# Queries as evicted serve head B's scores: mask rows on both halves, keys written from PSUM into the operands, and a planner that holds loads back

## The chip, the cores and the metric

The kernel runs on one core of a Trainium2 chip. The metric is the device time of one execution in microseconds (us), and the number that counts is the median over the runs. The engines are TensorE (PE; PEld is its weight load), VectorE (DVE), ScalarE (ACT), GpSimd (POOL) and SyncE (SP), which here only issues DMAs.

## The reference

Two stages. First an attention over blocks: q, k and v are [4, 8, 768, 64] in float32 (4 batches, 8 heads, 768 positions, width 64). Keys are averaged over blocks of 64; each query scores the 12 block means, and keeps the three best among the blocks that are not ahead of its own, and its own block. Ordinary causal softmax attention then runs over the kept blocks alone:

```
gate = q . mean(k, block of 64);  sel = top 3 of the causal blocks, and the own block
attn = softmax(where(sel & causal, q.k / 8, -1e9)) v
```

Then the heads are put side by side (x is [4, 768, 512]) and go through a gated long convolution over the sequence:

```
x1, x2, x3 = split(x @ w_proj)                    # w_proj [512, 1536]
y = x1 * irfft(rfft(x2) * rfft(filter)) * x3      # along the 768 positions
out = y @ w_out                                   # [4, 768, 512] float32
```

The Fourier transforms are done as matmuls with sine tables.

## The kernel before, in words

**Groups.** The work is 16 groups of two heads (A and B, `t` = 0 and 1), four groups to a batch. `prep(g)` makes a group ready, `attn(g)` does its attention, `hyena(b)` does the convolution of a batch once its four groups are through. Work of several groups runs interleaved.

**What `prep` does.** SP loads q, k (two transfers each) and v. PE transposes k and q in 128x128 pieces (L480, L517) into PSUM, so that the 64 partitions 0 to 63 hold head A and 64 to 127 head B, with the 768 positions along the row. DVE sums the blocks of keys (L485), ACT casts the keys to fp16 into `k2` (L490), POOL splits the sums in a high and a low half (`km`, L498, L499). ACT writes the scaled queries in fp16 as `q2h` (L522), DVE what rounding left as `q2l` (L527). PE multiplies both with `km` (the gate, L548). DVE finds the third largest of each row and writes a 0/1 mask (`sel`, L560 to L576); PE transposes the mask (L584); DVE copies it out of PSUM (L588).

**The operands of the scores.** A "slot" holds a group's score operands, and there are four slots. `Kt[i]` and `Qt[i]` are [128, 2, 768] in fp16; head `t` is the plane `[:, t, :]`, of which rows 0 to 63 are keys or queries and rows 64 to 75 the mask: in `Kt` a fixed pattern (-30720 where the row's number is the key's block, written once, L294), in `Qt` the mask of the group (L588). A matmul over 76 rows then gives the score and, where a block is not kept, a large negative number beside it (L606). The planes need head B's keys and queries on partitions 0 to 63, while the transposes left them on 64 to 127; and `k2` and `q2h` are used by the gate too. So both heads are copied into the planes: for the first six groups (`direct=6`) POOL copies the keys (L505, two to a group) and DVE the queries (L535, two to a group); from the seventh on SP moves both with DMAs from SBUF to SBUF (L503, L533, four to a group).

**What `attn` does.** For each head, PE computes scores into six PSUM banks (L606), ACT takes the exponential (L614), POOL zeroes above the diagonal (L625, "tri"), PE multiplies with v and a column of ones (L636, "pv"), DVE divides (L647, L648) into `xn`. `xn` is then folded by POOL (L676) and Fourier transformed by PE (L682); and its transpose goes to `xT`, for the first four groups (`xpe=4`) by PE with a DVE copy (L664, L670), later by a DMA transpose that SP issues (L655).

**What `hyena` does.** PE multiplies the transform with the middle of w_proj ("w2", L718), DVE with the filter's transform (L727), POOL combines (L732 to L748), PE transforms back (L788) and computes x1 and x3 from `xT` (L764); DVE and POOL multiply (L777, L800, L806); PE multiplies with w_out (L817), ACT or DVE evicts (L824), SP stores. Before the first `hyena`, the filter is loaded (six SP transfers, L374), POOL adds and subtracts its halves (six TENSOR_TENSOR, L382 and L385, "the six sums"), PE transforms it (L399, L406).

**What sets the order.** Nothing is scheduled on the chip. `Graph.schedule` (L104) is a planner that runs in Python: every operation has an engine, a duration that is written beside it, a priority and its dependencies, and the planner takes in turn the one that can start first, smaller priority first. What comes out is the order in which each engine's instructions are written, and an engine runs them strictly in that order, waiting where an operand is not there. SP's transfers are in the plan too, with `dma_free`, the time at which it believes the DMA queues to be empty. Group g is to start at `T(g)` = 9 + 13.6 g us, its `prep` 1.75 groups ahead. `f_at`, and the `after=` of the weight loads that POOL issues (L429, L434), say from which planned time on a load may go.

## Time and profile before

| | |
|---|---|
| runs | 261.70, 259.53 and 261.67 us; median 261.67 |
| the profiled execution | 259.5 us, of which the span from the first to the last instruction is 257.8 |
| mean granted TensorE clock | 0.975 of full speed |
| busy, us | PE 231.6, DVE 181.1, ACT 177.4, POOL 181.7, PE's weight loads 148.6 |
| DMA | 35.55 MB moved, 138 GB/s over the span |

The busy times are shares of one whole execution. PE is busy for 90% of the span; the 10% that are missing lie at the two ends: from about 79 us to 240 us PE hardly stops. Numbers behind a row in the form "x12" are counts of instructions; "mean ns" is the mean of one; what stands last in a row of the groups is the idle time of that engine just ahead of these instructions, and who ended it.

### The profile page before, as it was taken

The page shows a single profiled execution, that of the slowest core. Times are in us where ns is not written, and L with a number is a line of the kernel's source. Part 1 is how long each engine was busy: PE and PEld are TensorE (multiplying, and loading weights), DVE is VectorE, ACT ScalarE, POOL GpSimd, SP SyncE. Part 2 cuts the span into 40 slices and gives each one's busy share as a digit, 9 for nine tenths or more (in the row PEclk, how much of TensorE's full clock was granted, in tenths as well). Part 3 has the DMA queues.
Part 4 walks back from the last instruction along what each step waited for, and adds up shares of the span by engine and source line. Part 5 has one row for each costly group of instructions (what it writes and reads, how often), then busy time and mean ns, then how long its engine had stood idle before and what let it go on. Part 6 is the DMA issues. An engine that isn't in the chain of part 4 may idle for free.

```text
span 257.8 us, 6443 instructions
## 1 busy us (share of the span) xinstructions
PE 231.6 (90%) x2255; PEld 148.6 (58%) x2255; DVE 181.1 (70%) x564; ACT 177.4 (69%) x420; POOL 181.7 (70%) x273
## 2 busy tenths in 40 slices
PE   8778942997799999999999999999999999999971
PEld 4456722566476666667556657676655666455420
DVE  7789998359999876677749857767687446872422
ACT  7899980996687866958867966689759774033520
POOL 7556899196696899883917997675659978476550
PEclk9999985899999999999999999999999999999998
DMA  8999999999888293997887729302632011000435
GB/s 163 218 219 213 288 180 222 202 219 164 194 185 109 53 205 85 159 212 144 207 215 199 154 64 157 82 11 65 197 137 36 0 33 31 3 0 0 164 126 202
DMA packets 94272, 35.55 MB, mean 138 GB/s; under 512 B 85792, under 2 KB 90400, under 8 KB 94240
## 3 DMA queue, kind: packets, MB, share of 16 engines
q1 hardware_dynamic: 92128, 33.04, 60.7%
q0 software_dynamic: 2112, 2.10, 5.2%
q8 instruction: 18, 0.29, 0.5%
q14 instruction: 14, 0.11, 0.1%
HBM read 24.64 MB, written 6.29 MB: 120 GB/s over the span
## 4 chain that ended last, share of the span: by engine, by line
PE 52%; DVE 17%; POOL 13%; issue 8%; ACT 7%; DMA 1%; SPq 0%; DVEq 0%; POOLq 0%; ACTq 0%
PE ps L764 11%; PE ps L606 7%; PE ps L718 7%; PE ps L817 5%; PE ps L636 5%; PE ps L788 4%; PE ps L682 4%; POOL Y L748 3%; POOL ex L625 3%; ACT ex L614 2%; PE ps L517 2%; DVE m L568 2%; DVE Qt L588 2%; DVE Qt L535 2%; DVE q2l L527 2%
## 5 line engine op out<-in xcount | busy, mean ns | idle before, releaser
L614 ACT ACTIVATE ex<-ps 128x512 f16<-128x512 f32 x192 | 91.8, 603 | 14.8 <-PE ps L606 12.6
L606 PE MATMUL ps<-Qt,Kt 76*128 76x512 f16 (+3 forms) x256 | 49.3, 308 | 1.8 <-DVE Qt L588 0.8
L764 PE MATMUL ps<-xT,wp 128*128 128x384 f16 x256 | 46.8, 326 | 0.1
L625 POOL TENSOR_SCALAR_AFFINE_SELECT ex<-ex 128x384 f16<-128x384 f16 x64 | 32.4, 522 | 19.3 <-ACT ex L614 17.8
L636 PEld LDWEIGHTS <-ex 128*128 128x128 f16 x672 | 28.2, 98 | 12.7 <-POOL ex L625 4.7
L806 POOL TENSOR_TENSOR yT<-prod,sd 128x768 f16<-128x768 f32 x16 | 28.9, 1812 | 9.0 <-DVE sd L800 7.9
L636 PE MATMUL ps<-va,ex 128*128 128x65 f16 x672 | 31.2, 194 | 2.4 <-POOL ex L625 1.6
L676 POOL TENSOR_TENSOR xeo<-xn 128x384 f16<-128x384 f16 x32 | 28.5, 910 | 5.3 <-DVE xn L648 5.3
L764 PEld LDWEIGHTS <-wp 128*128 128x128 f16 x256 | 23.7, 97 | 14.0 <-issue 0.2
L606 PEld LDWEIGHTS <-Kt 76*128 76x128 f16 x256 | 23.0, 98 | 15.0 <-issue 2.3
L773 ACT CAST x<-ps 128x384 f16<-128x384 f32 x32 | 16.0, 505 | 20.7 <-PE ps L764 12.6
L490 ACT CAST k<-ps 128x384 f16<-128x384 f32 x32 | 15.9, 534 | 16.1 <-DVE ks L485 8.9
L777 DVE TENSOR_TENSOR prod<-ps,x 128x384 f32<-128x384 f32 x32 | 17.1, 553 | 12.8 <-ACT x L773 8.1
L800 DVE TENSOR_TENSOR sd<-ce,ps 128x384 f32<-128x384 f32 x32 | 16.3, 548 | 13.8 <-ACT ce L795 12.2
L817 PE MATMUL ps<-wo,yT 128*128 128x512 f16 x96 | 23.2, 379 | 1.8 <-POOL yT L806 1.7
L718 PE MATMUL ps<-wp,Xf 128*128 128x512 f16 x96 | 23.0, 379 | 0.1
L527 DVE SCALAR_TENSOR_TENSOR q2l<-ps,q2h 128x384 f16<-128x384 f32 x32 | 16.7, 551 | 6.0 <-ACT q2h L522 5.8
L682 PE MATMUL ps<-F,xeo 128*128 128x384 f16 x96 | 20.0, 326 | 0.3 <-DVE q2l L527 0.2
L727 DVE TENSOR_TENSOR t<-ps,HA 128x512 f32<-128x512 f32 x24 | 16.4, 684 | 3.9 <-PE ps L718 3.0
L824 ACT COPY osb<-ps 128x512 f32<-128x512 f32 x21 | 12.8, 613 | 9.0 <-issue 3.8
L788 PE MATMUL ps<-G,Y 128*128 128x384 f16 x96 | 18.9, 326 | 0.0
L648 DVE TENSOR_TENSOR xn<-ps,rec 128x384 f16<-128x384 f32 x32 | 17.8, 557 | 1.2
(99 smaller groups left out, 433.2 us busy)
## 6 DMA issues: line engine op xcount, KB each, us to landing
kn<-in_k_dram SPq DMA_DIRECT2D x32, 192.0 KB, 4.4
qn<-in_q_dram SPq DMA_DIRECT2D x32, 192.0 KB, 4.5
vn<-in_v_dram SPq DMA_DIRECT2D x16, 384.0 KB, 5.1
out_dram<-osb SPq DMA_DIRECT2D x24, 256.0 KB, 2.3
Kt<-k SPq DMA_DIRECT2D x20, 96.0 KB, 3.2
Qt<-q2h SPq DMA_DIRECT2D x20, 96.0 KB, 3.1
t<-in_moe_filter_fft_dram SPq DMA_DIRECT2D x6, 256.0 KB, 5.2
wp<-in_moe_w_proj_dram POOLq DMA_DIRECT2D x3, 512.0 KB, 8.6
```

The lines of the kernel that those rows point to most:

```text
L527: X.nc.vector.scalar_tensor_tensor(out=X.q2l[q2l.slot][:, cs], in0=X.ps(ps)[:, 0:HS], scalar=QS, in1=X.q2h[q2h.slot][:, cs], op0=ALU.mult, ...
L606: X.nc.tensor.matmul(X.ps(ps)[:, col:col + w], lhsT=kt[0:76, t, P * kc:P * (kc + 1)], rhs=qt[0:76, t, q0:q0 + w], start=True, stop=True, s ...
L614: X.nc.scalar.activation(X.ex[ex.slot][:, 512 * i:512 * i + w], X.ps(ps)[:, 0:w], AF.Exp, scale=ESC)
L625: X.nc.gpsimd.affine_select(out=dv, in_=dv, compare_op=ALU.is_ge, fill=0.0, base=0, pattern=[[0, 3], [1, P]], channel_multiplier=-1)
L636: X.nc.tensor.matmul(pt[:, 65 * c:65 * c + 65], lhsT=X.ex[ex.slot][:, w:w + P], rhs=X.va[va.slot][:, t, kc, :], start=(kc == 0), stop=(kc ...
L676: X.nc.gpsimd.tensor_tensor(X.xeo[xeo.slot][:, z, :], v[:, 0:HS], v[:, HS:S], op=a)
L682: X.nc.tensor.matmul(X.ps(ps)[:, 0:HS], lhsT=X.xeo[xeo.slot][:, z, P * t:P * (t + 1)], rhs=X.F[:, t, HS * z:HS * (z + 1)], start=(t == 0), ...
L718: X.nc.tensor.matmul(X.ps(ps), lhsT=l, rhs=X.wp[:, j, Dm:2 * Dm], start=(j == 0), stop=(j == DC - 1))
L764: X.nc.tensor.matmul(X.ps(ps)[:, 0:HS], lhsT=X.wp[:, d2, Dm * base + P * dc:Dm * base + P * (dc + 1)], rhs=X.xT[xT.slot][:, d2, hs:hs + HS ...
L788: X.nc.tensor.matmul(X.ps(ps)[:, 0:HS], lhsT=X.Y[Y.slot][:, 3 * par + n_, P * dc:P * (dc + 1)], rhs=X.G[:, 3 * par + n_, :], start=(n_ == ...
L806: X.nc.gpsimd.tensor_mul(X.yT[yT.slot][:, dc, :], X.prod[prod.slot], X.sd[sd.slot])
L817: X.nc.tensor.matmul(X.ps(ps), lhsT=X.yT[yT.slot][:, d2, P * c:P * (c + 1)], rhs=X.wo[:, d2, :], start=(d2 == 0), stop=(d2 == DC - 1), ski ...
```

## The change

- **One set of operands for both uses.** `Kt`, `Qt`, `k2` and `q2h` go. A slot now has `KA`, `QA` for head A and `KB`, `QB` for head B, each [128, 768] fp16. ACT writes the queries of both heads from PSUM into `QB` (L522): head B's are on rows 64 to 127, where `QB` wants them, and head A's are on rows 0 to 63. The gate reads `QB` too. Head A's queries are copied from `QB` into `QA`: for the first four groups (`direct=4`) by POOL, later by one DMA (L532, L535 of the changed kernel).
- **Mask rows on either side.** `QA` has its mask on rows 64 to 75, as before. `QB` has it on rows 0 to 11, over head A's queries, once these have been copied and the gate has read them (new memset L589, copy L590). `KB` has the fixed pattern on rows 0 to 11 and zeros on the rest of rows 0 to 63, so that what is left of head A's queries counts for nothing. Head B's score matmuls go over 128 rows, head A's over 76 as before. The two halves of `km` and of the mask change places to fit.
- **Keys from PSUM into the operands.** ACT casts head A's half (64 partitions) into `KA`, DVE head B's into `KB` (L496). The copies and DMAs of the keys go.
- **The planner** lets no SP transfer go while it believes the queues to be more than 2.7 us behind. This adds no wait to the program: it changes the order in which SP issues.
- **Numbers.** `xpe=0`: all 16 transposes to `xT` go by DMA. The filter is loaded from planned time 26 us on instead of 14; the weights from T(2.0), T(2.6), T(2.7) and T(3.6) on instead of T(1.0), T(1.6), T(1.7) and T(2.6).

```diff
@@ schedule
+                    if o.dma is not None and e == SP:
+                        t = max(t, dma_free - 2700.0)
                     t = max(t, f)
@@
-POOLS = dict(ps=8, slot=4, kn=3, qn=3, vn=2, va=3, k2=2, q2h=2, q2l=2, ks=2, km=3, nmp=2, m8=2,
+POOLS = dict(ps=8, slot=4, kn=3, qn=3, vn=2, va=3, q2l=2, ks=2, km=3, nmp=2, m8=2,
@@
-def build(X, tau=13.6, ahead=1.75, lag=1.5, direct=6, xpe=4, fill_to=13.0, f_at=14000):
+def build(X, tau=13.6, ahead=1.75, lag=1.5, direct=4, xpe=0, fill_to=13.0, f_at=26000, w_at=2.0):
...
         def qz(i=i):
-            X.nc.vector.memset(X.Qt[i][64:76, :, 0:P], 0.0)
-        op(DVE, 130, qz, w=[tok("slot0", i)], prio=-97 + 0.1 * i)
+            X.nc.vector.memset(X.QA[i][64:76, 0:P], 0.0)
+            X.nc.vector.memset(X.KB[i][0:64, :], 0.0)
+        op(DVE, 500, qz, w=[tok("slot0", i)], prio=-97 + 0.1 * i)
...
-            def kc(cs=cs, ps=ps):
-                X.nc.scalar.copy(X.k2[k2.slot][:, cs], X.ps(ps)[:, 0:HS])
-            op(ACT, act_n(HS), kc, r=[(ps, 0)], w=[(k2, hf)], prio=pr)
+            for t in range(2):
+                def kc(cs=cs, ps=ps, t=t):
+                    r = slice(64 * t, 64 * t + 64)
+                    (X.nc.vector.tensor_copy if t else X.nc.scalar.copy)(
+                        (X.KB if t else X.KA)[sl.slot][r, cs], X.ps(ps)[r, 0:HS])
...
-        for t in range(2):
-            def ksh(t=t):
-                X.nc.sync.dma_start(X.Kt[sl.slot][0:64, t, :], X.k2[k2.slot][64 * t:64 * t + 64, :])
-            def kcp(t=t):
-                X.nc.gpsimd.tensor_copy(X.Kt[sl.slot][0:64, t, :], X.k2[k2.slot][64 * t:64 * t + 64, :])
...
-        for t in range(2):
-            def qsh(t=t):
-                X.nc.sync.dma_start(X.Qt[sl.slot][0:64, t, :], X.q2h[q2h.slot][64 * t:64 * t + 64, :])
-            def qcp(t=t):
-                X.nc.vector.tensor_copy(X.Qt[sl.slot][0:64, t, :], X.q2h[q2h.slot][64 * t:64 * t + 64, :])
...
+        def qsh():
+            X.nc.sync.dma_start(X.QA[sl.slot][0:64, :], X.QB[sl.slot][0:64, :])
+
+        def qcp():
+            X.nc.gpsimd.tensor_copy(X.QA[sl.slot][0:64, :], X.QB[sl.slot][0:64, :])
+        e = (POOL, 850, qcp) if g < direct else (SP, 450, qsh)
+        op(*e, r=[(sl, "q", 0), (sl, "q", 1)], w=[(sl, "qA")], dma=None if g < direct else 430,
+           prio=pr + 40, name="qA")
...
             def mcp(t=t):
-                X.nc.vector.tensor_copy(X.Qt[sl.slot][64:76, t, P:S],
-                                        X.ps16(mt)[64 + 32 * t:76 + 32 * t, 0:S - P])
+                r = slice(64 - 64 * t, 76 - 64 * t)
+                if t:
+                    X.nc.vector.memset(X.QB[sl.slot][r, 0:P], 0.0)
+                X.nc.vector.tensor_copy((X.QB if t else X.QA)[sl.slot][r, P:S], X.ps16(mt)[r, 0:S - P])
...
-               w=[(sl, "m", t)], prio=pr + 60, name="mcp")
+               w=[(sl, "m", t)] + ([(sl, "q", 0), (sl, "q", 1), (sl, "qA")] if t else []),
+               prio=pr + 60, name="mcp")
...
                 def qk(bank=bank, ps=ps, t=t):
-                    kt, qt = X.Kt[sl.slot], X.Qt[sl.slot]
+                    kt, qt = (X.KB, X.QB) if t else (X.KA, X.QA)
+                    r = slice(0, P if t else 76)
                     for (col, kc, q0, w) in bank:
                         X.nc.tensor.matmul(X.ps(ps)[:, col:col + w],
-                                           lhsT=kt[0:76, t, P * kc:P * (kc + 1)],
-                                           rhs=qt[0:76, t, q0:q0 + w], start=True, stop=True,
+                                           lhsT=kt[sl.slot][r, P * kc:P * (kc + 1)],
+                                           rhs=qt[sl.slot][r, q0:q0 + w], start=True, stop=True,
```

How the order moves is shown at three places. The first is DVE, where the fourth group's selection stands. Before (`Qt_81` is the fourth slot; the digits are buffer numbers):

```order
L527 SCALAR_TENSOR_TENSOR q2l_105<-ps_62,q2h_103 128x384
L527 SCALAR_TENSOR_TENSOR q2l_105<-ps_65,q2h_103 128x384
L535 COPY Qt_81<-q2h_103 64x768 x2
L560 MEMSET ps_68 64x5x2
L561 MEMSET ps_68 128x2x8
L562 MEMSET ps_68 128x2x6
L568 MAX m_1_114<-ps_68 128x8 x10
```

and with the change:

```order
L489 TENSOR_REDUCE ks_111<-ps_66 128x6
L496 CAST KB_81<-ps_66 64x384
L527 SCALAR_TENSOR_TENSOR q2l_109<-ps_68,QB_89 128x384
L527 SCALAR_TENSOR_TENSOR q2l_109<-ps_64,QB_89 128x384
L559 MEMSET ps_64 64x5x2
L560 MEMSET ps_64 128x2x8
L561 MEMSET ps_64 128x2x6
L567 MAX m_1_118<-ps_64 128x8 x10
```

The two copies of the queries between the rounding rest and the selection are gone; a cast of the keys stands ahead instead.

The second is POOL, around the six sums of the filter. Before:

```order
L505 COPY Kt_77<-k_1_101 64x768
L382 TENSOR_TENSOR Y_138<-t_130,t_131 128x512
L385 TENSOR_TENSOR Y_138<-t_130,t_131 128x512
L382 TENSOR_TENSOR Y_138<-t_132,t_133 128x512
L385 TENSOR_TENSOR Y_138<-t_132,t_133 128x512
L382 TENSOR_TENSOR Y_138<-t_134,t_135 128x512
L385 TENSOR_TENSOR Y_138<-t_134,t_135 128x512
L505 COPY Kt_77<-k_1_101 64x768
L625 AFFINE_SELECT ex_115<-ex_115 128x3x128 x2
```

and with the change:

```order
L535 COPY QA_85<-QB_89 64x768
L681 TENSOR_TENSOR xeo_128<-xn_125 128x384 x2
L507 CAST km_112<-ks_111 64x12
L508 TENSOR_TENSOR km_112<-ks_111,km_112 64x12
L507 CAST km_112<-ks_111 64x12
L508 TENSOR_TENSOR km_112<-ks_111,km_112 64x12
L630 AFFINE_SELECT ex_119<-ex_119 128x3x128 x2
L387 TENSOR_TENSOR Y_142<-t_134,t_135 128x512
L390 TENSOR_TENSOR Y_142<-t_134,t_135 128x512
L387 TENSOR_TENSOR Y_142<-t_136,t_137 128x512
```

The sums still stand in one run of six, now behind the diagonal mask of a head instead of ahead of it.

The third is SP, behind the six loads of the filter. Before:

```order
L374 DMA t_135<-in_moe_filter_fft_dram 128x512
L454 DMA vn_96<-in_v_dram 128x12x64
L447 DMA kn_91<-in_k_dram 128x6x64 x2
L447 DMA qn_94<-in_q_dram 128x6x64 x2
L447 DMA kn_89<-in_k_dram 128x6x64 x2
L447 DMA qn_92<-in_q_dram 128x6x64
```

and with the change:

```order
L379 DMA t_139<-in_moe_filter_fft_dram 128x512
L660 DMA_TRANSPOSE xT_130<-xn_125 128x6x128
L452 DMA kn_99<-in_k_dram 128x6x64
L452 DMA qn_102<-in_q_dram 128x6x64 x2
L660 DMA_TRANSPOSE xT_130<-xn_126 128x6x128
L532 DMA QA_82<-QB_86 64x768
L459 DMA vn_104<-in_v_dram 128x12x64
L452 DMA kn_97<-in_k_dram 128x6x64 x2
```

Two transposes, of the first and the second group (`xn_125`, `xn_126`), now stand ahead of loads and of the first copy into `QA` by DMA.

More of the change, by code (lines that the diff above doesn't have):

```diff
@@ L282, in etiny @@
         gp = X.nc.gpsimd
-        e = X.et[64:76, :]
-        gp.memset(e, EMASK)
-        gp.affine_select(out=e, in_=e, compare_op=ALU.is_equal, fill=0.0, base=0,
-                         pattern=[[1, NB]], channel_multiplier=-1)
-    op(POOL, 400, etiny, w=[tok("et")], prio=-99.5, name="etiny")
+        gp.memset(X.et, EMASK)
+        for r in (0, 64):
+            e = X.et[r:r + 12, :]
+            gp.affine_select(out=e, in_=e, compare_op=ALU.is_equal, fill=0.0, base=0,
+                             pattern=[[1, NB]], channel_multiplier=-1)
+    op(POOL, 600, etiny, w=[tok("et")], prio=-99.5, name="etiny")
     for i in range(POOLS["slot"]):
         def qz(i=i):
-            X.nc.vector.memset(X.Qt[i][64:76, :, 0:P], 0.0)
-        op(DVE, 130, qz, w=[tok("slot0", i)], prio=-97 + 0.1 * i)
+            X.nc.vector.memset(X.QA[i][64:76, 0:P], 0.0)
+            X.nc.vector.memset(X.KB[i][0:64, :], 0.0)
+        op(DVE, 500, qz, w=[tok("slot0", i)], prio=-97 + 0.1 * i)
         for t in range(2):
             def ebc(i=i, t=t):
+                r, dst = ((64, X.KA), (0, X.KB))[t]
                 (X.nc.vector.tensor_copy if i >= 2 else X.nc.scalar.copy)(
-                    X.Kt[i][64:76, t, :].rearrange("p (n s) -> p n s", s=64),
-                    X.et[64:76, :].rearrange("p (n o) -> p n o", o=1).to_broadcast([12, NB, 64]))
-            op(*((DVE, 470) if i >= 2 else (ACT, 700)), ebc, r=[tok("et")],
+                    dst[i][r:r + 12, :].rearrange("p (n s) -> p n s", s=64),
+                    X.et[r:r + 12, :].rearrange("p (n o) -> p n o", o=1).to_broadcast([12, NB, 64]))
+            op(*((DVE, 470) if i >= 2 else (ACT, 700)), ebc, r=[tok("et"), tok("slot0", i)],
                w=[tok("slot1", i, t)], prio=-90 + t if i == 0 else T(i - ahead) - 1000)
@@ L424, in build @@
     Hall = [tok("H", c, k) for c in range(HC) for k in range(2)] + [tok("HA0")]
-    for part, when in ((1, 1.0), (0, 1.6), (2, 1.7)):
+    for part, when in ((1, w_at), (0, w_at + 0.6), (2, w_at + 0.7)):
         def lw(part=part):
@@ L434, in lo @@
         X.nc.gpsimd.dma_start(X.wo, X.wosrc)
-    op(POOL, 1100, lo, w=[tok("wo")], dma=3600, prio=T(2.6), after=T(2.6), name="lwo")
+    op(POOL, 1100, lo, w=[tok("wo")], dma=3600, prio=T(w_at + 1.6), after=T(w_at + 1.6), name="lwo")
     slots, vas = {}, {}
@@ L487, in prep @@
             op(DVE, dve_n(HS), red, r=[(ps, 0)], w=[(ks, hf)], prio=pr)
-            def kc(cs=cs, ps=ps):
-                X.nc.scalar.copy(X.k2[k2.slot][:, cs], X.ps(ps)[:, 0:HS])
-            op(ACT, act_n(HS), kc, r=[(ps, 0)], w=[(k2, hf)], prio=pr)
+            for t in range(2):
[3 more added lines that the diff above has]
+                        (X.KB if t else X.KA)[sl.slot][r, cs], X.ps(ps)[r, 0:HS])
+                op(*((DVE, dve_n(HS)) if t else (ACT, act_n(HS))), kc,
+                   r=[(ps, 0)] + (slot_c if g >= POOLS["slot"] else [tok("slot0", g)]),
+                   w=[(sl, "k", t, hf)], prio=pr + 20 * t, name="kc")
         def kms():
@@ L883 @@
     X.et = one("et", [P, NB], FP16)
-    X.Kt = [one(f"Kt_{i}", [P, 2, S], FP16) for i in range(POOLS["slot"])]
-    X.Qt = [one(f"Qt_{i}", [P, 2, S], FP16) for i in range(POOLS["slot"])]
+    for name in ("KA", "KB", "QA", "QB"):
+        setattr(X, name, [one(f"{name}_{i}", [P, S], FP16) for i in range(POOLS["slot"])])
     X.F, X.G = one("F", [P, HC, S], FP16), one("G", [P, 6, HS], FP16)
@@ L893 @@
     many("va", [P, 2, NQ, 65], FP16)
-    for name in ("k2", "q2h", "q2l"):
-        many(name, [P, S], FP16)
+    many("q2l", [P, S], FP16)
     many("ks", [P, NB], FP32)
```

38 lines of the change are left out of this document (15 added, 23 removed).

## The prediction

> **What bounds the kernel now.** I read the page's slices first, then the busy times of stretches, then the waits and the timeline of the worst stretch. In the slices (6.4 us each, tenths) PE is full from the thirteenth on, and has its deepest hole in the sixth and seventh:
>
> ```profile
> PE   8778942997799999999999999999999999999971
> PEclk9999985899999999999999999999999999999998
> ```
>
> The stretches put numbers on it (columns: stretch, its length, then busy us of PE, PEld, DVE, ACT, POOL; PEclk, DMA share, GB/s):
>
> ```profile
> 0.00:34.80 34.80, 29.19 (x305) 19.37 (x305) 29.44 (x101) 31.92 (x70) 24.23 (x61) 1.00 1.13 220
> 34.80:43.30 8.50, 0.57 (x4) 0.31 (x3) 8.04 (x19) 2.58 (x6) 8.36 (x10) 0.62 0.96 201
> 43.30:60.00 16.70, 16.51 (x157) 11.35 (x158) 9.33 (x19) 14.77 (x36) 10.51 (x19) 0.88 1.11 198
> 60.00:78.40 18.40, 15.44 (x247) 11.44 (x246) 16.70 (x75) 13.09 (x35) 12.78 (x29) 1.00 0.92 186
> 78.40:240.00 161.60, 159.48 (x1499) 101.70 (x1498) 112.53 (x345) 110.25 (x269) 120.05 (x155) 1.00 0.49 101
> 240.00:257.80 17.80, 10.38 (x50) 4.47 (x48) 5.11 (x9) 4.84 (x10) 5.81 (x4) 0.93 0.48 178
> ```
>
> In the chain that ended last the first w2 matmul (L718) stands at 78.48:
>
> ```profile
> 78.48 0.86 PE ps L718 x4
> ```
>
> From there to 240 us PE idles 2.1 us of 161.6: PE is the bound, and nothing that other engines gain there shortens it. Before that the bound changes: ACT until 34.8 (31.92 of 34.8), then nobody useful for 8.5 us, then PE and ACT, then DVE (16.70 of 18.4). So the time of the kernel is the moment at which w2 starts, plus 161.6, plus the tail of 17.8. The change is worth what it moves that moment by.
>
> The hole has one cause. PE stands before the mask of the fourth group, which it is to transpose; the waits name DVE (total, times, longest), and the timeline has the one long wait:
>
> ```profile
> PE ps L584 <- DVE nmp L576: 8.7, 2, 7.9
> ```
>
> ```profile
> 43.31 0.71 PE L584 MATMUL ps<-id,nmp 128*128 128x128 f16 x5 [7.95 <-DVE nmp L576]
> ```
>
> On DVE, two copies of queries come just ahead of that mask and take 9.12 us together:
>
> ```profile
> 32.28 9.12 DVE L535 COPY Qt<-q2h 64x768 f16<-64x768 f16 x2
> 41.40 0.07 DVE L560 MEMSET ps<- 64x10 f32 x1
> ```
>
> Of the twelve such copies the shortest takes 342 ns, and one 8215 (minimum, median, maximum):
>
> ```profile
> L535 DVE COPY Qt<-q2h x12: 342/694/8215, 9.9 to 58.9; 64x768 f16<-64x768 f16 x12
> ```
>
> While the long one lasts POOL runs the six sums with no gap:
>
> ```profile
> 32.91 1.26 POOL L382 TENSOR_TENSOR Y<-t,t 128x512 f16<-128x512 f32 x1
> ...
> 39.02 1.25 POOL L385 TENSOR_TENSOR Y<-t,t 128x512 f16<-128x512 f32 x1
> 40.34 0.84 POOL L505 COPY Kt<-k 64x768 f16<-64x768 f16 x1
> ```
>
> The copy ends 1.1 us after the run does. I read it as held by POOL: both go from SBUF to SBUF. A DVE copy that reads PSUM is never held (minimum, median, maximum of the 32 copies of masks):
>
> ```profile
> L588 DVE COPY Qt<-ps x32: 489/492/497, 15.0 to 189.5; 12x640 f16<-12x640 f16 x32
> ```
>
> The Trainium skill (SBUF — State Buffer, "SBUF: two separate sides") says that DVE in a two-port mode and GpSimd share a pair of ports as an exclusive lock for the whole instruction. The trace agrees on the holding but not on its length: 8.2 us went over six POOL instructions, not one of 1.26.
>
> **The change part by part.** The sum is made against the profiled execution: span 257.8, time 259.5. That is the fast one of the runs shown (259.53); their median, 261.67, is 0.8% above it, so I cannot forecast a median to better than about 2 us, and about 1% is also what a measurement of this kernel can tell from no change.
>
> *The held copies go* (L535), and no DVE instruction that is left in the loop copies from SBUF to SBUF. The order of DVE above shows it: the rounding rest is followed by the selection at once. PE's wait of 7.9 us goes: **-7.9**. Bounds: -7.9 if the sums, which still run for 7.3 us on POOL, let everything else pass; -0.6 if PE's next work had to wait for all of them, through a diagonal mask behind them. I take the first, because now the mask of the second group's last head stands ahead of the sums, and PE has the score matmuls of over two heads to do before it needs either the sums or the next mask.
>
> A second pair is held at 58.3 us (2.67 for two where 0.68 is free), where DVE is the bound:
>
> ```profile
> 58.30 2.67 DVE L535 COPY Qt<-q2h 64x768 f16<-64x768 f16 x2
> ```
>
> Between 0 and -2.0, since PE idles 2.96 us in that stretch: **-1.5**.
>
> *The slow clock goes with the hole.* After it PE works for 3.9 us at half clock:
>
> ```profile
> 43.30:47.20 3.90, 3.89 (x18) 2.97 (x19) 2.70 (x6) 2.00 (x5) 1.35 (x2) 0.51 1.20 187
> ```
>
> That is 1.9 us of matmul time at most; ACT is nearly full right behind it, so little of it reaches w2: **-0.5** (0 to -1.9).
>
> *PE's own transposes go*, and with them four DVE copies (L670):
>
> ```profile
> L664 PE MATMUL ps<-id,xn 128*128 128x128 f16 x24 | 2.0, 220 | 0.5 <-DVE xn L648 0.4
> ```
>
> These 2.0 us lie before w2, where PE is not the bound: **-0.3** (0 to -2.0).
>
> *Work that DVE takes on.* Half of the key casts: 32 of 64x384 from PSUM to fp16. Nearest rows are DVE's and ACT's of 384 columns from PSUM:
>
> ```profile
> L485 DVE TENSOR_REDUCE ks<-ps 128x6 f32<-128x384 f32 x32 | 17.2, 552 | 1.8 <-PE ps L480 1.0 <-ACT k L490 0.4
> L535 DVE COPY Qt<-q2h 64x768 f16<-64x768 f16 x12 | 16.5, 1371 | 0.1
> L670 DVE COPY xT<-ps 128x768 f16<-128x768 f16 x4 | 2.2, 557 | 1.8 <-ACT HA L414 1.7
> L257 DVE MEMSET prod<- 128x384 uint32 x1 | 0.4, 378 | 0.0
> L290 DVE MEMSET Qt<- 12x128 uint32 x4 | 0.6, 165 | 0.1
> ```
>
> At 0.55 each that is 17.6 us, half of it (8.8) before w2; sixteen small memsets (L589) of at most 0.17 are up to 2.6 more, half before w2. Removed before w2: twelve copies at their free 0.34 (4.1 us) and 2.2 of L670. DVE is busy 63.5 us up to 78.4; without 12.4 us of holding 51.1; with the new work about 56, of some 69.5. That leaves a fifth idle: **+0.5** (0 to +4.5, if all of it fell on the chain). Behind w2 DVE goes from 112.5 to about 122 of 161.6, under a full PE: 0 (to +3).
>
> *Zeros in KB* are four memsets of at most 0.38 at the start, 1.5 us ahead of the first key sum. The first gate waited for an ACT sine (L347) and not for DVE, and two copies go from there:
>
> ```profile
> PE ps L548 <- ACT F L347: 1.1, 1, 1.1
> ```
>
> ```profile
> 9.95 1.83 DVE L535 COPY Qt<-q2h 64x768 f16<-64x768 f16 x2
> ```
>
> **+0.3** (0 to +0.8, the zeros less half of these copies).
>
> *POOL* gives up twelve copies of 0.82 and takes four of the same shape: -6.6 us on an engine that is not the bound: 0. The score matmuls over 128 rows instead of 76 change nothing (379 against 387 ns for 512 columns in full-height and 76-row groups):
>
> ```profile
> L505 POOL COPY Kt<-k 64x768 f16<-64x768 f16 x12 | 9.9, 821 | 3.4 <-ACT k L490 2.9
> L606 PE MATMUL ps<-Qt,Kt 76*128 76x512 f16 x96 | 29.6, 387 | 0.9 <-DVE Qt L588 0.8
> L718 PE MATMUL ps<-wp,Xf 128*128 128x512 f16 x96 | 23.0, 379 | 0.1
> ```
>
> *SP.* 40 copies by DMA become 12, and four transposes join. Early on the DMA queues are full (share 1.13 in the first 34.8 us), but not late: the eleventh group's keys were sent for at 69 us, and PE needs eight before w2. What costs is SP's order: it is strict, and a transpose waits for `xn`. In the new order the second group's transpose stands ahead of the fifth group's copy into `QA`, of v and of the seventh group's keys. That `xn` was ready at 52 us, so about 44 now. A load lands 4.4 us after its issue, a copy 3.1. (Below, from the timeline: that `xn`, PE's transpose of the seventh group's keys, SP's issue of the eleventh's; then medians from issue to landing.)
>
> ```profile
> 51.58 0.56 DVE L648 TENSOR_TENSOR xn<-ps,rec 128x384 f16<-128x384 f32 x1
> ```
>
> ```profile
> 57.98 0.55 PE L480 MATMUL ps<-id,kn 128*128 128x128 f32 x3
> ```
>
> ```profile
> 68.96 2.17 SPq L447 DMA_DIRECT2D kn<-in_k_dram  x2
> ```
>
> ```profile
> kn<-in_k_dram SPq DMA_DIRECT2D x32, 192.0 KB, 4.4
> Qt<-q2h SPq DMA_DIRECT2D x20, 96.0 KB, 3.1
> wp<-in_moe_w_proj_dram POOLq DMA_DIRECT2D x3, 512.0 KB, 8.6
> ```
>
> The seventh group's keys would be there at about 50; PE took them at 58 before, so it asks for them at about 50 now: **+0.7** (0 to +3). The later weights and the limit on loads only reorder; the first weights are needed at 70 us and land 8.6 us after an issue at some 45: 0.
>
> *A new wait on DVE.* The memset and copy into `QB` wait until `QA` has been copied out of it. From the fifth group on that is a DMA of 0.6 + 3.1 us behind the last query eviction. The selection chain that stands between (0.55 for the rest L527, 0.6 for the gate, 1.9 from the first memset at 41.40 to PE's transpose at 43.31, 0.7 for that) is about as long:
>
> ```profile
> 107.27 0.62 PE ps L548 x19
> ```
>
> So 0. If it is late, all of DVE queues behind it, and PE behind DVE; see the last rival.
>
> Sum: -7.9 - 1.5 - 0.5 - 0.3 + 0.5 + 0.3 + 0.7 = **-8.7**. Span 249.1, time **250.8 us**. All good ends together give -13.8 (245.7 us), all bad ones +10.7 (270.2).
>
> **The rivals.**
> 1. *SP's order eats half*: the queue stands before the two transposes, loads and the `QA` of the fifth and sixth group come late, PE waits about 4 us before w2. For it: SP waits for `xn` in the profile, up to 12.2 us at once; against it: two groups of slack. 254.8 us. Chance 0.18.
>
> ```profile
> SPq L655 <- DVE xn L648: 21.2, 4, 12.2
> SPq L828 <- ACT osb L824: 38.8, 14, 23.3
> ```
>
> 2. *More is freed than I count*: clock, second hold and PE's transposes come through in full, -12: 247.5 us. For it: PE's idle time before w2 is 16.7 us in all; against it: ACT is busy 62.4 us before w2 and must still do that. Chance 0.12.
> 3. *The long copy was held by something else.* If a hold ends with the POOL instruction that is running (1.26 us), 6.6 of the 8.2 us have another cause that the change may leave: 259.5 - 8.7 + 6.6 = 257.4 us. It is the reading that the section of the Trainium skill cited above would give. Against it: the end of the copy lies at the end of the run. Chance 0.05.
> 4. *Slower: DVE at the head of its line.* The memset for `QB` waits for the `QA` transfer in twelve groups, and that transfer stands behind SP's waits for `xn` and `osb`, 60 us in all. If a quarter of these came to stand before a `QA` copy, and DVE's idle time (49 us of 161.6) did not cover them, 15 us would be added: 265.8 us. It decides from 8.7 us on, 0.73 us in each of the twelve groups. Chance 0.07.
>
> **How the numbers follow.** The forecast has 0.58, the rivals 0.18, 0.12, 0.05 and 0.07. The range 246.5 to 256.5 reaches from the second rival to a little past the first, and leaves out the last two and the tails. Faster by over 1% (below 259): forecast, second rival, nearly all of the first: 0.87. Within 1%: the third and a mishap in the first: 0.06. Slower: 0.07.
>
> **What would show it right or wrong.** Right: no DVE instruction above 1.5 us; PE's hole of 8 us gone and the granted clock 1.0 throughout slices 6 to 9; first w2 at 69 to 71 us; then about 161 us with PE idle for some 2 of them. Wrong: PE or DVE waiting for a DMA into `QA` or for `kn`; a wait behind the six sums (L387, L390) of over 3 us; w2 before 67 or after 75 us; PE idle over 5 us after w2.

## The result and the profile after

The change takes **254.37 us** (median of four runs, 253.57 to 254.59) against 261.59 for the kernel before in the same call: a ratio of 0.974, 95% interval 0.968 to 0.979, which is 6.9 us, or 5.5 to 8.3. The forecast was 250.8 us, with a range of 246.5 to 256.5. The profiled execution took 253.57 us with a span of 251.5; the one on which the sum was made took 259.53 with 257.8. So the profiled pair is 6.3 us apart in span where the sum said 8.7.

The kernel before comes out at two levels from run to run, about 259.5 and about 262 us, with spans of 257.8 and 260.5 and a mean granted clock of 0.977 and 0.962; below, kernels are therefore compared by their medians and by the stretches of their profiled executions, and differences under 1 us are not read.

The slices of the profile's page after, to be set against the first fence of the prediction:

```profile
PE   7689898989899899999999999999999999999971
PEclk9999999999999999999999999999999999999999
```

The hole in the sixth and seventh slice is gone, and the clock with it no longer falls. The second of the stretches as before, then the two from the new first w2 product on (stretch, length, busy us of PE, PEld, DVE, ACT, POOL, granted clock, DMA share, GB/s):

```profile
34.80:43.30 8.50, 7.51 (x76) 4.79 (x72) 6.28 (x27) 8.34 (x22) 7.77 (x7) 1.00 0.91 164
69.04:234.00 164.96, 161.14 (x1517) 102.57 (x1515) 124.43 (x375) 110.10 (x268) 119.08 (x153) 1.00 0.51 103
234.00:251.50 17.50, 10.51 (x51) 4.54 (x48) 5.10 (x9) 4.96 (x10) 5.93 (x4) 1.00 0.48 180
```

In the 8.5 us of the hole PE works 7.51 us where it worked 0.57. In the chain that ended last the first w2 product now stands here:

```profile
69.04 1.73 PE ps L723 x8
```

That is 9.44 us earlier than at 78.48. But from there to the end it takes 182.5 us (164.96 + 17.50) and not 179.3. Of the three parts of the prediction's formula (moment of w2, 161.6, tail) the first gave 0.7 us more than forecast, and the other two together took 3.1 us back. Not all of that is lost time: one group's gate matmuls and query transposes (behind w2, 180 and 54 matmuls where there were 160 and 48) stood ahead of w2 before and stand behind it now, by their rows about 2 us. In the long stretch PE is busy 1.7 us more (161.14 against 159.48) and idle 1.7 us more (3.8 against 2.1). PE's longest waits behind w2 name DVE, but for one (total, times, longest):

```profile
PE ps L611 <- DVE KB L496: 1.1, 2, 0.8
PE ps L583 <- DVE nmp L575: 0.5, 1, 0.5
PE ps L641 <- ACT x L778: 0.5, 1, 0.5
```

and the new rows on DVE are of the size that was forecast (busy us, mean ns, idle ahead):

```profile
L496 DVE CAST KB<-ps 64x384 f16<-64x384 f32 x32 | 17.4, 559 | 0.7
L589 DVE MEMSET QB<- 12x64 uint32 x16 | 1.8, 112 | 0.7
L294 DVE MEMSET KB<- 64x384 uint32 x4 | 1.5, 378 | 0.5
```

In this execution neither PE nor DVE waits for a transfer into `QA` or for keys.

### The profile page after: what moved, and what is told of

The parts are those of the page before. It is cut to its first block, busy times and chain, and to the rows that moved or that the text cites. A ratio compares the mean times of both kernels' runs of the same rounds, so it can differ in the third digit from the quotient of the medians.

```text
span 251.5 us, 6371 instructions
## 1 busy us (share of the span) xinstructions
PE 231.2 (92%) x2231; PEld 145.6 (58%) x2231; DVE 184.1 (73%) x600; ACT 177.3 (70%) x420; POOL 174.6 (69%) x266
## 4 chain that ended last, share of the span: by engine, by line
PE 47%; DVE 27%; POOL 8%; ACT 8%; issue 7%; DMA 1%; SPq 0%; DVEq 0%; ACTq 0%; POOLq 0%
PE ps L769 12%; PE ps L723 7%; PE ps L611 5%; PE ps L687 5%; PE ps L793 4%; PE ps L822 4%; ACT ex L619 4%; DVE KB L496 4%; DVE m L567 3%; PE ps L641 3%; DVE ks L489 3%; DVE q2l L527 2%; POOL xeo L681 2%; DVE xn L653 2%; DVE QB L590 2%
## 5 line engine op out<-in xcount | busy, mean ns | idle before, releaser
L619 ACT ACTIVATE ex<-ps 128x512 f16<-128x512 f32 x192 | 89.9, 579 | 14.5 <-PE ps L611 12.3
L611 PE MATMUL ps<-QB,KB 128*128 128x512 f16 (+3 forms) x128 | 26.5, 305 | 1.9 <-DVE KB L496 1.1
L611 PE MATMUL ps<-QA,KA 76*128 76x512 f16 (+3 forms) x128 | 24.2, 305 | 2.7 <-DVE QA L590 1.1
L489 DVE TENSOR_REDUCE ks<-ps 128x6 f32<-128x384 f32 x32 | 17.1, 551 | 3.2 <-PE ps L484 2.3
L527 DVE SCALAR_TENSOR_TENSOR q2l<-ps,QB 128x384 f16<-128x384 f32 x32 | 16.6, 553 | 2.3 <-ACT QB L522 1.9
L496 ACT CAST KA<-ps 64x384 f16<-64x384 f32 x32 | 14.6, 490 | 5.1 <-PE ps L484 3.8
```

The lines of the kernel that those rows point to most:

```text
L496: (X.nc.vector.tensor_copy if t else X.nc.scalar.copy)((X.KB if t else X.KA)[sl.slot][r, cs], X.ps(ps)[r, 0:HS])
L611: X.nc.tensor.matmul(X.ps(ps)[:, col:col + w], lhsT=kt[sl.slot][r, P * kc:P * (kc + 1)], rhs=qt[sl.slot][r, q0:q0 + w], start=True, stop=True,
L619: X.nc.scalar.activation(X.ex[ex.slot][:, 512 * i:512 * i + w], X.ps(ps)[:, 0:w], AF.Exp, scale=ESC)
```

## The experiments

### The hold alone (e1_act_copy)

The kernel before, with nothing changed but the engine of the fourth group's two copies:

```
-                X.nc.vector.tensor_copy(X.Qt[sl.slot][0:64, t, :], ...)
+                (X.nc.scalar.copy if g == 3 else X.nc.vector.tensor_copy)(
+                    X.Qt[sl.slot][0:64, t, :], ...)
```

> The kernel before, with one thing else: the two query copies of the fourth group (L535, one of which took 8.2 us) are issued by ACT at the place in the program where DVE had them; the order of everything else is the same. Theory (POOL's run of six sums holds DVE's SBUF-to-SBUF copy): PE's wait for the fourth group's mask falls from 7.95 us to under 1.5, no DVE copy is over 3 us, first w2 at 71 to 73 us, time 252.5 to 255 against 259.5 to 261.7. Rival (the run of sums keeps PE waiting anyway, through the diagonal masks and the filter's transform behind it): the wait goes to a line that needs POOL, first w2 at 76 us or later, time 257.5 or more.

Measured: 251.86 us (251.81 to 253.34), ratio 0.969 (0.963 to 0.974) to 259.63 in its call: 7.8 us, a little more than the theory had. PE transposes the fourth group's mask at 38.69 us, with no wait for DVE, where it was 43.31. The two copies take 0.83 us each on ACT, and the ten left on DVE are never held for long (minimum, median, maximum ns):

```profile
L535 DVE COPY Qt<-q2h x10: 342/459/972, 9.9 to 54.3; 64x768 f16<-64x768 f16 x10
L535 ACT COPY Qt<-q2h x2: 829/830/832, 33.7 to 35.0; 64x768 f16<-64x768 f16 x2
```

Its stretches from its first w2 product on:

```profile
72.24:233.90 161.66, 159.50 (x1499) 101.82 (x1498) 112.71 (x345) 110.41 (x269) 120.42 (x155) 1.00 0.52 106
233.90:251.60 17.70, 10.35 (x50) 4.42 (x47) 5.10 (x9) 4.80 (x10) 5.77 (x4) 0.91 0.48 179
```

Behind w2 it is the kernel before to a tenth (161.66 and 17.70), and w2 stands 6.1 us earlier (72.40 in the chain that ended last, where it was 78.48). (This profiled run is the slowest of its four by 1.5 us.) So the first term of the sum is shown: taking the held pair off DVE is worth 7.8 us by itself. It also shows that two lines do more than the whole change: no run of the change (253.44 at best) reached the slowest of this kernel (253.34). The rest of the change costs 2 to 3 us net.

### What holds DVE, measured by itself (e7_holds, e10_holds)

Two kernels that compute nothing of the reference and store zeros: in each stage POOL gets a run of instructions and DVE one instruction beside it. The core of a stage of the second, where a short ACT copy ahead of DVE's release puts DVE behind POOL's start:

```
pool()                                      # 0, 1, 3 or 6 sums; six masks, copies, fp16 sums
act.copy(w16[:, 0:256], z16[:, 0:256])
act.copy(dst[:, 0:8], z[:, 0:8])
vec.tensor_copy(dst[0:64, :], src[0:64, :]) # or a cast from PSUM, a memset, ...
```

> A small kernel by itself; it computes nothing of the reference and stores zeros. In each stage POOL is given a run of instructions and DVE, about 0.2 us later, one instruction, all starting from the same ACT write; each stage is done twice. DVE copy of 64x768 fp16 from SBUF to SBUF: with nothing on POOL 0.34 us. Theory (held until POOL's back-to-back run ends): about 1.3 us beside one sum (128x512 float32 in, 1.26 us each), 3.8 beside three, 7.5 beside six, about 3.2 beside six diagonal masks (0.52 each). Rival (held for the one POOL instruction in progress): at most 1.6 us beside any number. Beside six sums: a cast from PSUM of 64x384 0.25 to 0.56 us, a memset of 64x768 0.4, rounding rest (PSUM and SBUF in) 0.55, all unheld by both; an addition of two SBUF inputs of 384 columns held like the copy.

In the first, DVE's copy came behind the start of a sum in one stage only (beside one sum: 1.42 us, which both theories allow); in the other stages with sums it started ahead of POOL and ran in its free 0.35 us, so it could not tell the two apart. Beside six masks it came 0.09 us behind their start, and was held:

```profile
25.89 0.64 DVE L122 COPY dst<-src 64x768 f16<-64x768 f16 x1 [9.02 <-ACT dst L95]
25.80 3.01 POOL L71 TENSOR_SCALAR_AFFINE_SELECT y<-y 128x384 f16<-128x384 f16 x6 [1.71 <-ACT a L93]
```

> A kernel of its own, which stores zeros and computes nothing of the reference: in each stage POOL gets a run of instructions back to back and DVE one instruction about 0.6 us later. DVE's copy of 64x768 from SBUF to SBUF (0.35 us alone) beside 1, 3 and 6 POOL sums (fp32 128x512, about 1.2 us each), six masks, six POOL copies, six fp16 sums; then beside six sums a cast from PSUM, a memset, an operation with one PSUM and one SBUF source, and an add of two SBUF operands. Theory (the DVE copy is held for as long as POOL's run goes on without a gap): about 1.0, 3.4 and 7.0 us beside 1, 3 and 6 sums. Rival (it is held until the POOL instruction under way ends): at most 1.1 us beside each of the three.

Measured in the second, DVE's instructions in order of their stages (start, us): beside nothing, 1, 3 and 6 sums, six masks, six POOL copies, six fp16 sums; then beside six sums a cast from PSUM, a memset, an operation with one PSUM and one SBUF source, and an add of two SBUF operands:

```profile
6.08 0.35 DVE L114 COPY dst<-src 64x768 f16<-64x768 f16 x1 [0.86 <-ACT dst L107]
8.54 1.12 DVE L119 COPY dst<-src 64x768 f16<-64x768 f16 x1 [2.11 <-ACT dst L107]
11.82 1.18 DVE L124 COPY dst<-src 64x768 f16<-64x768 f16 x1 [2.17 <-ACT dst L107]
17.45 1.18 DVE L129 COPY dst<-src 64x768 f16<-64x768 f16 x1 [4.45 <-ACT dst L107]
26.73 0.35 DVE L134 COPY dst<-src 64x768 f16<-64x768 f16 x1 [8.10 <-ACT dst L107]
30.22 0.42 DVE L139 COPY dst<-src 64x768 f16<-64x768 f16 x1 [3.14 <-ACT dst L107]
34.20 0.73 DVE L144 COPY dst<-src 64x768 f16<-64x768 f16 x1 [3.56 <-ACT dst L107]
40.02 0.55 DVE L149 CAST dst<-ps 64x384 f16<-64x384 f32 x1 [5.09 <-ACT dst L107]
49.29 0.38 DVE L154 MEMSET dst<- 64x384 uint32 x1 [8.72 <-ACT dst L107]
58.35 0.56 DVE L159 SCALAR_TENSOR_TENSOR dst<-ps,src 128x384 f16<-128x384 f32 x1 [8.68 <-ACT dst L107]
67.52 1.18 DVE L164 TENSOR_TENSOR dst<-src,e 128x384 f16<-128x384 f16 x1 [8.61 <-ACT dst L107]
```

and POOL's runs of one, three and six sums, the six masks, the six copies and the six fp16 sums:

```profile
8.18 1.26 POOL L69 TENSOR_TENSOR y<-a,b 128x512 f16<-128x512 f32 x1 [7.67 <-ACT a L104]
11.53 3.81 POOL L69 TENSOR_TENSOR y<-a,b 128x512 f16<-128x512 f32 x3 [2.08 <-ACT a L104]
17.15 7.47 POOL L69 TENSOR_TENSOR y<-a,b 128x512 f16<-128x512 f32 x6 [1.81 <-ACT a L104]
26.33 3.03 POOL L81 TENSOR_SCALAR_AFFINE_SELECT y<-y 128x384 f16<-128x384 f16 x6 [1.71 <-ACT y L103]
29.82 3.51 POOL L73 COPY y<-h 64x512 f16<-64x512 f16 x6 [0.47 <-ACT y L103]
33.81 5.35 POOL L77 TENSOR_TENSOR y<-h 128x384 f16<-128x384 f16 x6 [0.48 <-ACT y L103]
```

The copy is held, and it ends 0.22 us after the *first* sum (8.18 + 1.26 = 9.44; the copy ends at 9.66), whether one, three or six sums are queued. The rival (one instruction) is right here and my theory (the whole run) is not. The section of the Trainium skill that the prediction cites (SBUF — State Buffer, "SBUF: two separate sides") has a lock for the whole instruction, and these rows agree with it: 1.26 us of a sum, and not 7.47 of six. Beside sums, a copy from SBUF to SBUF (0.35 alone) and an add of two SBUF operands take 1.12 to 1.18 us; a cast from PSUM (0.55), a memset (0.38) and an operation with one PSUM source (0.56) are not held, which is what the prediction took from L588.

The rows beside POOL's other work fit the same rule. With the mean of one POOL copy (0.63 us), one fp16 sum (0.92) and one mask (0.54), the DVE copies that took 0.42 and 0.73 us, and the 0.64 of the first small kernel, end about 0.2 us after the first POOL instruction of their run too. The 0.35 beside masks says nothing against it: that copy came 0.40 us into a mask, and its free end (27.08) is also where the hold would have let it go (26.33 + 0.54 + 0.2).

So the 8.2 us of the kernel before stay unexplained in their length. (The prediction's 1.1 us between the end of POOL's run and the end of the copy is that of the pair; the long copy itself ends 0.22 us after the run.) Its rows in that stretch, POOL's copy ahead of the sums and DVE's first copy by itself:

```profile
32.13 0.82 POOL L505 COPY Kt<-k 64x768 f16<-64x768 f16 x1
```

```profile
32.28 8.21 DVE L535 COPY Qt<-q2h 64x768 f16<-64x768 f16 x1
```

It came while POOL was in a copy, and ended at 40.49, again 0.22 us after POOL's sixth sum (39.02 + 1.25 = 40.27); the second copy then ended at 41.40, 0.22 after POOL's next copy (40.34 + 0.84 = 41.18). The same end, then, but six chances were lost that the small kernel's DVE took at the first. What differs (a POOL copy under way when DVE's turn came, two operations in turn on POOL, a copy into other partitions in the second of the pair) was not told apart by any run.

### The casts of head B's keys (e8_no_casts, e2_casts_act, e9_casts_in_e1)

The change without the casts into `KB` for the last eight groups. These groups score head B with older keys; that is the part of the computation left out.

```
+                    if t and g >= 8:
+                        return
                     (X.nc.vector.tensor_copy if t else X.nc.scalar.copy)(
```

> The change with head B's key casts on DVE (L496, 0.56 us each) left out for groups 8 to 15: 16 DVE instructions, about 9 us of DVE, all behind the first w2 product; those groups score head B with older keys, which is the part of the computation that is left out. Theory (DVE's added casts are why PE now idles 3.8 us behind the first w2 product where it idled 2.1 before): PE's idle time there falls to 2.0 to 2.6 and the kernel is 1.5 to 2.5 us faster than the change's 254.4, so 252 to 253. Rival (the added casts lie under a full PE, as predicted, and the idle time comes from the order): within 0.5 us of the change, 253.9 to 254.9.

Measured: 252.34 us (251.47 to 253.63), ratio 0.969 (0.963 to 0.975), 2.0 us below the change's 254.37, which was measured in another call. Its stretches from its first w2 product on:

```profile
69.79:232.00 162.21, 159.84 (x1517) 102.97 (x1516) 115.63 (x360) 109.57 (x268) 119.01 (x153) 1.00 0.51 104
232.00:249.50 17.50, 10.52 (x51) 4.51 (x48) 5.09 (x9) 4.97 (x10) 5.95 (x4) 0.93 0.48 180
```

From w2 to the end 179.7 us: of the change's 182.5, 2.8 go with 8.8 us of DVE's work (2.9 if both are cut at the moment in the chain that ended last, 69.96 us here). PE's idle time in the long stretch falls from 3.8 us (164.96 - 161.14) to 2.4 (162.21 - 159.84), inside what the theory gave. The other 1.3 us are less busy PE time for the same 1517 recorded matmuls; waits too short for a view would look so, but no view shows them. The order of PE is the same in both, so it is the casts and not the order that cost. DVE lies idle a quarter of that stretch (124.43 of 164.96 busy), and still they cost a third of their length.

Where they cost it can be read between two rows of PE that are the same in both kernels, the transposes of a mask at 82.15 and 90.94 us in the change (L583), and at 83.06 and 90.44 here (L585):

```profile
82.15:90.94 8.79, 7.17 (x84) 4.80 (x81) 8.09 (x31) 5.35 (x15) 5.62 (x10) 1.00 1.29 223
```

```profile
83.06:90.44 7.38, 6.85 (x84) 4.78 (x81) 6.78 (x29) 4.58 (x14) 5.79 (x10) 1.00 1.23 224
```

DVE is busy for 92% of the 8.79 us of the change; the two casts in it (1.1 us) make it 1.4 us longer. From there to the mask at 182.40 us (180.41 here) the other casts are 7.6 us of DVE's time and cost 1.5.

The casts of those groups on ACT in place of DVE:

```
-                    (X.nc.vector.tensor_copy if t else X.nc.scalar.copy)(
+                    (X.nc.vector.tensor_copy if t and g < 8 else X.nc.scalar.copy)(
```

> The change, with head B's key casts of the last eight groups (L496, 16 of 0.56 us on DVE) issued by ACT in the same places. Theory (behind the first w2, DVE's new casts cost the PE idle time, 3.8 us where it was 2.1): PE idle from the first w2 to 234 us falls to about 2.3, time 1 to 2 us below the change's 254.4. Rival (PE idles more there because w2 now starts earlier against the other engines' work, whatever DVE has to do): idle stays at 3.5 or more, time within 0.5 us of the change.

Measured: 255.66 us (255.07 to 256.41), ratio 0.982 (0.977 to 0.988): 1.3 slower than the change, which neither theory had. PE idles more behind w2, 5.4 us against 3.8:

```profile
69.93:236.70 166.77, 161.37 (x1517) 103.11 (x1516) 115.53 (x360) 117.51 (x284) 119.24 (x153) 1.00 0.49 101
```

So giving the work to the other engine that evicts is no cure; it does not tell DVE's share from ACT's.

The casts added to the first experiment's kernel and nothing else, ACT and DVE with half of the partitions each:

```
-                X.nc.scalar.copy(X.k2[k2.slot][:, cs], X.ps(ps)[:, 0:HS])
+                X.nc.scalar.copy(X.k2[k2.slot][0:64, cs], X.ps(ps)[0:64, 0:HS])
+                X.nc.vector.tensor_copy(X.k2[k2.slot][64:P, cs], X.ps(ps)[64:P, 0:HS])
```

> The kernel before with the two long copies on ACT (251.9 us when it ran), and in it each of the 32 pairs of key evictions split: ACT casts 64 partitions and DVE the other 64, which gives DVE the 32 added casts of about 0.55 us and ACT no less time, and leaves operands and waits as they were. Theory (the added DVE casts are the cost that the prediction counted as nothing): 1.5 to 3 us slower than 251.9, so 253.4 to 254.9, with DVE busy about 17 us longer. Rival (the layout, the order or the wait for the shared operand costs it): within 0.5 us of 251.9.

Measured: 263.19 us (262.94 to 264.80), ratio 1.009 (1.006 to 1.013): 11.3 us slower than that kernel, far beyond both theories. The casts are as long as in the change, but stand where the planner had put ACT's copy, and there DVE waits for ACT (last column):

```profile
L491 DVE CAST k<-ps 64x384 f16<-64x384 f32 x32 | 17.4, 560 | 4.5 <-ACT k L490 3.8
```

The edit added waits at the head of DVE's queue as well as work, so it gives no price for the work alone. What it shows is that 17.4 us of casts without a place in the plan cost 11 us; the half of them behind w2, placed by the plan, cost 2 to 3.

### The change's numbers (e5_old_times, e3_no_limit, e4_pe_transposes, e6_dve_qa, e11_numbers_on_before)

Each is the change with one number put back. A second measurement of the change itself stood beside them.

> The changed kernel once more, on the same chip as the three that undo a part of it: 253.5 to 254.6 us.

Measured: 254.69 us (253.44 to 255.98), ratio 0.979 (0.972 to 0.985): wider than expected, with the median 0.3 us above the first.

*The filter and weight loads at their old times:*

```
-def build(X, ..., f_at=26000, w_at=2.0):
+def build(X, ..., f_at=14000, w_at=1.0):
```

> The change with the old times of the loads (filter from planned 14 us, weights from T(1.0) on). The six sums then stand earlier on POOL and with other work between them, and 1 MB of weights is asked for ahead of keys and queries. Theory (with no SBUF-to-SBUF copy left on DVE, it does not matter where the sums stand; the queues are what is full early): 0 to 2 us slower than the change. Rival (the later loads only put the filter's transform closer to w2): 0.5 to 2 us faster.

Measured: 258.11 us (257.06 to 258.25), ratio 0.991 (0.987 to 0.994): 3.4 slower than the change beside it, more than the theory's 2 and against the rival. I had counted the later weights at 0 and given the filter's later load no term. The first w2 product stands 7 us earlier than in the change, and yet the kernel ends later:

```profile
61.98:237.80 175.82, 170.06 (x1622) 107.74 (x1619) 134.43 (x423) 117.20 (x285) 123.29 (x165) 1.00 0.49 104
```

Here the order itself is another (1622 matmul records behind w2, not 1517), so the moment of w2 no longer measures progress: it is a clock only between kernels whose orders put the same work behind it. Of the 3.9 us between the profiled spans (255.4 and 251.5) only 1.0 is PE's idle time (21.3 against 20.3, span less busy). One wait between 43 and 60 us is new, for POOL's fold of `xn` (`xeo`), which the change does not have there:

```profile
PE ps L687 <- POOL xeo L681: 1.5, 3, 0.7
```

The rest shows as PE busy for longer with the same work (234.1 against 231.2), with the granted clock at 1.00 up to the tail in both; where it lies stays open.

*No limit on SP's loads:*

```
-                    if o.dma is not None and e == SP:
-                        t = max(t, dma_free - 2700.0)
```

> The change without the planner's limit on loads (SP's order alone is planned anew). Theory (the queues have slack before the first w2, so SP's order costs and brings little): within 1 us of the change. Rival (the limit is what keeps the copies into QA and the keys from standing behind loads): 2 us or more slower, with PE or DVE waiting for QA or kn.

Measured: 254.04 us (253.35 to 256.93), ratio 0.978 (0.970 to 0.986). Three runs lie at 253.4 to 254.1; the profiled one took 256.93, and it has the waits that the rival spoke of, for transfers into `QA` and for keys:

```profile
DVE QB L587 <- DMA QA<-QB: 4.5, 1, 4.5
PE ps L609 <- DMA QA<-QB: 1.7, 1, 1.7
PE ps L482 <- DMA kn<-in_k_dram: 1.4, 1, 1.4
```

So by the median the limit brings nothing, but without it DVE's new wait for a transfer into `QA` can be a long one. Whether the faster runs had such waits is not known, since one execution was profiled.

*PE's own transposes back:*

```
-def build(X, ..., direct=4, xpe=0, ...):
+def build(X, ..., direct=4, xpe=4, ...):
```

> The change with the first four groups' transposes on PE again (xpe=4: 24 matmuls, 2.0 us, and four DVE copies, 2.2 us, before the first w2; four transposes less on SP). Theory (PE and DVE have idle time before w2): within 1 us of the change. Rival one (PE's and DVE's work there is worth its own length): 2 us slower. Rival two (SP standing before transposes costs more than that): 1 to 3 us faster.

Measured: 254.05 us (252.44 to 254.50), ratio 0.975 (0.969 to 0.981). By their medians neither of these two can be told from the change (254.4 and 254.7).

*The copies into `QA` on DVE in the first four groups:*

```
-            X.nc.gpsimd.tensor_copy(X.QA[sl.slot][0:64, :], X.QB[sl.slot][0:64, :])
+            X.nc.vector.tensor_copy(X.QA[sl.slot][0:64, :], X.QB[sl.slot][0:64, :])
```

> The change, with the four query copies into QA (L535) issued by DVE in the places where POOL had them, so that SBUF-to-SBUF copies on DVE are back. Theory (any such copy is held while POOL works, until POOL's run ends): of the four copies at least two take over 0.7 us where a free one takes 0.34, as long as what POOL has in hand then; but none stands beside the six sums, so none takes 8 us, and the time stays within 1.5 us of the change's 254.4. Rival (only the long run of sums matters, shorter POOL work holds nothing): all four at 0.34 to 0.5 us.

Measured: 256.89 us (256.50 to 257.07), ratio 0.986 (0.980 to 0.992): 2.2 to 2.5 slower than the change, but not by a hold. The copies lie between the two expectations, and none takes over 0.7 us:

```profile
L535 DVE COPY QA<-QB x4: 352/514/692, 11.1 to 33.0; 64x768 f16<-64x768 f16 x4
```

The sums stand at another place beside them, so this did not try the long hold. Half of what its profiled execution lost, it lost at the start (columns as in the stretches above, granted clock third from the end):

```profile
8.00:12.00 4.00, 1.83 (x9) 0.42 (x6) 3.91 (x8) 3.71 (x9) 1.71 (x5) 1.00 1.36 218
12.00:14.00 2.00, 1.70 (x25) 1.44 (x26) 1.48 (x13) 1.31 (x4) 0.00 (x0) 0.71 1.36 217
14.00:16.00 2.00, 2.00 (x9) 1.20 (x8) 1.70 (x9) 1.54 (x4) 0.00 (x0) 0.50 1.36 218
```

Behind a hole of PE the granted clock falls to 0.71 and 0.50, and the first transpose of a mask (L583) comes at 16.60 us and not at 14.73: 1.9 us. At w2 it is 3.8 (72.81 against 69.04). In between stands a wait for keys that the change's profile does not have:

```profile
PE ps L484 <- DMA kn<-in_k_dram: 1.2, 1, 1.2
```

*The change's numbers on the operands of before:* no shared operand, no casts on DVE, no new wait; query copies of the first four groups on POOL, the loads at the change's times, no limit.

```
-def build(X, ..., direct=6, xpe=4, fill_to=13.0, f_at=14000):
+def build(X, ..., direct=4, xpe=4, fill_to=13.0, f_at=26000):
-    for part, when in ((1, 1.0), (0, 1.6), (2, 1.7)):
+    for part, when in ((1, 2.0), (0, 2.6), (2, 2.7)):
...
-                X.nc.vector.tensor_copy(X.Qt[sl.slot][0:64, t, :], ...)
+                X.nc.gpsimd.tensor_copy(X.Qt[sl.slot][0:64, t, :], ...)
```

> The operands of the kernel before (no shared operand, no key casts on DVE) with the change's other numbers: direct=4, query copies of groups 0 to 3 on POOL, the filter and weight loads at the change's later times, xpe=4 and no limit on SP. If the long hold is gone with the copies and the later loads help as they do in the change, and the shared operand with its casts is what costs: 250 to 252.5 us, 2 to 4 faster than the change. Rival (the operand layout costs nothing, the order that these numbers give is what costs): 254 or more.

Measured: 254.76 us (252.61 to 256.53), ratio 0.975 (0.967 to 0.983): the median is the change's, and lies on the rival's side, but the runs are spread over both theories (without the slowest, the median is 254.42). With DVE at 114.50 us behind w2, ten less than in the change, PE idles 2.6 us there:

```profile
70.76:233.30 162.54, 159.92 (x1515) 102.02 (x1512) 114.50 (x349) 110.04 (x269) 118.87 (x153) 1.00 0.53 114
```

So the stretch behind w2 is cheap again without the casts, as in the kernel without them, and what is given back lies before w2, or in the spread from run to run: the profiled execution is the fastest of its four, which are 3.9 us apart. The later loads, worth 3.4 us in the change's order, are not a gain by themselves: the first experiment's kernel keeps the old times and is 2.6 to 2.9 us faster than this one. Terms of this kind do not add up; each changes the order for all the others.

## Why the prediction was right and where it was wrong

*Right: the held pair* (-7.9, and -0.5 for the clock behind it). Taken away alone it is worth 7.8 us, the wait for the mask is gone in both kernels, and the granted clock is 1.0 in slices 6 to 9. POOL's sums still run and nobody waits 3 us for them. *Not shown: why the hold was so long.* The text read it as a run of POOL instructions that keeps DVE out. In the small kernel a run does not do that. The forecast did not depend on it, because all copies from SBUF to SBUF left DVE's loop either way; a change that had only shortened the run would have rested on the unproved half.

*Right in its number, in part by luck: the moment of w2.* Forecast 69.8 (78.48 - 8.7), with 69 to 71 as the sign to look for; measured 69.04. But about 2 us of PE's work moved from ahead of w2 to behind it, which the sum did not foresee and which can bring w2 forward by as much; how much of the 9.4 us is owed to it no run shows. So that the terms ahead of w2 (second pair, PE's transposes, zeros, SP's order, DVE's casts at +0.5) hold as a sum is not shown. One by one they are mostly below what can be read: the transposes and, by the median, the limit on loads make no difference, and the second pair was hardly held in the first experiment (1.06 us for the two in place of 2.67) although it stayed on DVE, so its -1.5 was a matter of when and not of which engine.

*Wrong: "Behind w2 DVE goes from 112.5 to about 122 of 161.6, under a full PE: 0 (to +3)".* DVE went to 124.4 as forecast, but the step from there to nothing fails. The half of the casts behind w2 costs 2.8 us of the profiled stretches. (Of the 3.1 us by which w2 to the end grew, a part is the moved work, so the two numbers agree more closely than they should.) A mean of 75% is not cover: from 69 to 100 us DVE is busy nine tenths of the time, and there PE waits for its products:

```profile
69.00:100.00 31.00, 29.08 (x301) 19.38 (x298) 27.44 (x85) 21.22 (x54) 25.67 (x35) 1.00 1.22 206
```

Half of the cost falls in 9 us of this stretch, as the two rows of the experiment without casts show; the rest is spread over the 90 us behind it. The bound of +3 had the size; I took the lower end for the mean over 161.6 us, and did not look at the stretches in it.

*Wrong: the later loads at nothing.* The weights stood at 0 and the filter had no term. In this order the two are worth 3.4 us together; of that the profile names only the wait for POOL's fold (1.5 us).

*The sum.* The forecast of 250.8 is 3.6 us low against the median, of which the casts are 2.0 by the medians and 2.8 by the profiled stretches; the profiled span (251.5) is 2.4 above the forecast's 249.1: 3.1 more from w2 to the end, and 0.7 less ahead of it.

*The rivals.* The first (SP's order) and the fourth (DVE behind the transfer into `QA`) did not come: the change's profile has no wait for either transfer. The fourth was no empty fear, though: without the planner's limit, which the prediction counted at 0, one execution has it once, with 4.5 us. The second asked for 12 us ahead of w2; 9.4 came, the moved work included. The third is half right: one POOL instruction is what holds in the small kernel, but no other cause of the long copy was left in the changed one, so its time did not come. (Its 257.4 us also lies below 259, so its chance of 0.05 belonged to "faster by over 1%" and not to "within 1%".)

*Better than both.* The kernel before with two copies moved to ACT takes 251.9 us, 2.5 less than the change. Taken together, the change's other parts cost more than they bring.

## What to carry to other kernels

Look for one instruction that takes ten times its usual time before planning a new layout, and first try moving just that one to another engine: here this was worth the whole gain and more. When work is added to an engine "under" a full one, price it stretch by stretch and not by the mean; here two casts, 1.1 us together, cost 1.4 where DVE was busy for 92% of the time, and the next 7.6 us of casts cost 1.5. A marker such as the first product of a late stage measures progress only between kernels whose orders put the same work behind it; here about 2 us of work changed sides.
